# A spectral filter and a ReGLU block on one core: x loaded ahead of the weights, new due times in the head, transform stages in pairs, last columns in three parts

## The chip, the cores and the metric

The kernel runs on one core of a Trainium2 chip. The metric is the device time of one execution in microseconds (us); lower is better. The time before is the median of three runs, 411.16 us (410.84 to 411.76).

## The reference, cut to what matters

```python
def _A_ref(x, w_r, w_i):                      # S = 2048, D = 512
    X = rfft2(x, axes=(-2, -1)) * (w_r + 1j * w_i)
    return irfft2(X, s=(S, D), axes=(-2, -1))

def _B_ref(x, W_gate, W_up, W_down):          # F = 1376
    gate, up = x @ W_gate, x @ W_up
    h = gate * (gate > 0) * up
    return h @ W_down

xn = _layernorm(x)
s = _A_ref(xn, A_w_r, A_w_i)
g = _silu(_B_ref(xn, B_W_gate, B_W_up, B_W_down))
return x + s * g
```

All inputs are float32. Only A_x is used as x. The output is 2048 x 512.

## The kernel before, in words

**Arithmetic.** Every float32 operand of a large product is split into two float16 parts, a high and a low one, and a product is three passes (high by high, high by low, low by high). Weights are first scaled by a power of two that comes from their sum of squares.

**Tiles.** The 2048 rows of x are 16 slices of 128; two slices make a chunk (8 chunks), four make a block (4 blocks). F is cut into 11 tiles of 128 (the last has 96). Gate and up products of one tile of F and one block (`product`) are 12 matmuls of 512 columns into a "gu" PSUM buffer, of which there are two. ScalarE rectifies the gate half (`rectify`), VectorE multiplies it with the up half and splits the result (`hidden`), and the down product (`down`) adds 11 tiles of F for one slice, into a "dn" buffer. `gate` applies the silu on ScalarE.

**Head.** A block's products need its x transposed. For the first two chunks (slices 0 to 3) this is done early: load x (`load_x`), mean and variance on VectorE (`stats`), the reciprocal root (`deviation`: a small VectorE step, a root on ScalarE, a larger VectorE step), normalisation to `xf` (`normalise`), four TensorE transposes of each slice into the PSUM tile `head` (`turn_row`), a copy of the high part to `xT` on ScalarE and of the low part on VectorE. At the same time the weights come in groups (`load_group`, tile `raw`): ScalarE squares them (`squares`), a TensorE matmul with ones sums over partitions (`sum`), VectorE makes the scale `p` (`group_scale`), and the high part is written by ScalarE or VectorE and the low part by VectorE (`group_split`, tile `wgu`). Groups 0, 1 and 2 are one tile of F each. Block 0's first three tiles of F are done for slices 0 and 1 first (12 matmuls of 256 columns for each product), then for slices 2 and 3. Until there is work, TensorE runs dummy matmuls (`keep_busy`, tile `idle`): 60 steps, the first nine of three matmuls, the others of one.

**Transform.** Each chunk is folded (`fold`) and split (`split`), then a first stage of small 64 by 64 matmuls (`first_stage`, tile `s`, 24 matmuls, after which the result goes through DRAM), then eight filter chunks (`fft_chunk`, tiles y, xx, z, v), each with its part on ScalarE, VectorE and GpSimd (tiles `tt`, `po`, `pf`), again through DRAM, then a last stage per chunk (`last_stage`, 24 matmuls into `s`) and the unfolding on GpSimd and VectorE (tiles `ae`, `ye`, `sv`). `finish` multiplies by the silu, adds x and stores. The very last slice is cut by `columns` into two parts of 256 columns, so that the end of the first overlaps the matmuls of the second (tile `dn_3b`).

**What sets the order.** Nothing is issued in the order of the text. Each piece of work is a step of a planner (`Plan`), with an engine, an estimated cost, what it reads and writes, and a due time, its own or derived backwards from its users'. `Plan.run` places steps one by one, on each engine taking of the steps that can begin soonest the one with the earliest due time, with rooms for tiles, one DMA rate of 340 KB/us, 0.095 us for a change of the matmul's shape (`mode`), and a rule that steps marked `port` do not overlap between VectorE and GpSimd. The result is a fixed order for each engine, which the chip keeps. The constants ahead of the functions (T0, FIRST, MID, LAST and their steps, LOADS, LOADX, HIGH_ACT, NORM) are due times and choices of engine. In a trace almost all instructions have the line L64, where the wrapper `InOrder` issues them, so tiles tell them apart.

Of the kernel before, what the change touches and what calls it, by code (L numbers as in the profile page):

```python
# [14 lines left out]
P = 128  # L15
# [3 lines left out]
NCH = 8  # L19
# [51 lines left out]
class Plan:  # L71
# [159 lines left out]
def kernel(ctx: ExitStack, tc: tile.TileContext, x, w_in, wd, wd_tail, wl, ew, sp, c_r, c_d, c_m, c_x, c_s, out):  # L231
# [36 lines left out]
    warm = cpool.tile([P, 1], F32, name="warm")  # L268
    ACT.activation(warm, ones[:, 0:1], AF.Sqrt)
# [21 lines left out]
    def load_x(c):  # L291
        tile_of(f"x{c}", "k4", [P, 2, D], F32)
        for i in range(2) if c == 0 else [None]:
            rows = slice(2 * c, 2 * c + 2) if i is None else slice(i, i + 1)
            to = slice(0, 2) if i is None else slice(i, i + 1)
            step("SP", .6, lambda rows=rows, to=to: SP.dma_start(T[f"x{c}"][:, to], x[:, rows, :]),
                 writes=[(f"x{c}", i)], lead=14 if c else None, kb=512 if i is None else 256, lag=2.2, due=(LOADX[c] + (i or 0) * .01) if c < 2 else None)

    def x_names(c, i):
        return [(f"x{c}", None if c else i)]  # L300

    def stats(c, q, j):
# [7 lines left out]
        for i in range(2):  # L310
            step("DVE", .82, lambda i=i: run(i), reads=x_names(c, i), writes=[(f"st{c}", i), (f"mv{c}", i)])

    def deviation(c):
# [7 lines left out]
        def last():  # L321
# [32 lines left out]
    def normalise(c, q, at, engines=("DVE", "DVE")):  # L354
# [33 lines left out]
    def keep_busy(n):  # L388
# [65 lines left out]
    def first_stage(c, due):  # L454
# [12 lines left out]
        step("PE", SCOST, run, mode=1, reads=["cR", (f"xs16_{c}", 0), (f"xs16_{c}", 1)], writes=[f"s1_{c}"], due=due, margin=MARGIN)  # L467
# [730 lines left out]
```

## Time and profile before

| | before |
|---|---|
| median of 3 runs | 411.16 us (410.84 to 411.76) |
| the profiled execution | 410.83 us, of it 409.1 us span |
| matmuls | 402.5 us busy, 98% of the span |
| VectorE | 306.6 us, 75% |
| ScalarE | 190.0 us, 46% |
| GpSimd | 47.6 us, 12% |
| granted TensorE clock | 0.997 |
| moved by DMA | 51.72 MB |

The span runs from the first to the last instruction of the profiled execution; its device time is 1.7 us longer. PE is TensorE's matmuls, PEld its weight loads, DVE is VectorE, ACT ScalarE, POOL GpSimd, SP the engine that issues most DMAs (SPq its queue of instructions). A row of a timeline gives start, duration, engine, what is written and what is read, and in brackets the idle time before it with what ended it.

### The profile page before, as it was taken

Reading aid. Unit: us, or ns where it says so; the run is one execution under the profiler, and the core shown is the slowest. Engines: PE = TensorE matmul, PEld = TensorE weight load, DVE = VectorE, ACT = ScalarE, POOL = GpSimd, SP = SyncE. Lnnn points to the kernel's source line nnn. Section 1 sums busy time; section 2 is a strip of 40 time slices with the busy share of each in tenths; the row PEclk is TensorE's granted clock in tenths of the full one; section 3 lists DMA queues with packets and bytes.
Section 4 is the critical chain, followed back from the end, with each engine's and each line's share of the span. In section 5 each row is a group of like instructions: output and inputs, shape, how many; then the busy total and the mean of one; then the engine's idle time right before and its main releaser. Section 6 shows DMA issues by size and latency. Waiting matters only on the chain.

```text
span 409.1 us, 7662 instructions
## 1 busy us (share of the span) xinstructions
PE 402.5 (98%) x3023; PEld 213.4 (52%) x3023; DVE 306.6 (75%) x646; ACT 190.0 (46%) x359; POOL 47.6 (12%) x68
## 2 busy tenths in 40 slices
PE   8899999999999999999999999999999999999995
PEld 7784444544444444545465455556455445444554
DVE  3959999999999993515776977878863325999973
ACT  5999655435452549320445434536432327223321
POOL 0000000000000000001230312311311006133320
PEclk9999999999999999999999999999999999999998
DMA  8970210317138269753005144142322089656511
GB/s 285 416 253 6 98 49 3 92 64 154 44 111 145 59 182 355 209 170 116 2 0 168 34 135 125 58 155 57 115 51 53 0 192 221 210 177 211 176 53 52
DMA packets 34948, 51.72 MB, mean 126 GB/s; under 512 B 15392, under 2 KB 17024, under 8 KB 34912
## 3 DMA queue, kind: packets, MB, share of 16 engines
q1 hardware_dynamic: 34624, 50.71, 41.4%
q10 hardware_dynamic: 288, 0.52, 0.5%
q8 instruction: 23, 0.38, 0.4%
q14 instruction: 13, 0.11, 0.1%
HBM read 35.48 MB, written 12.60 MB: 118 GB/s over the span
## 4 chain that ended last, share of the span: by engine, by line
PE 98%; DVE 0%; ACT 0%; issue 0%
PE gu L64 55%; PE dn L64 27%; PE s L64 3%; PE z L64 3%; PE xx L64 3%; PE idle L64 2%; PE y L64 2%; PE v L64 2%; PE dn_3b L64 1%; PE head L64 0%; ACT xT L64 0%; PE sum L64 0%; DVE xT L64 0%; ACT g L64 0%; DVE sv L64 0%
## 5 line engine op out<-in xcount | busy, mean ns | idle before, releaser
L64 PE MATMUL gu<-xT,wgu 128*128 128x512 f16 (+1 forms) x1032 | 214.8, 364 | 1.2 <-ACT xT L64 1.0
L64 PEld LDWEIGHTS <-wgu 128*128 128x128 f16 x1032 | 99.4, 98 | 105.0 <-issue 4.6
L64 PE MATMUL dn<-wds,h 128*128 128x512 f16 (+2 forms) x528 | 115.5, 373 | 0.0
L64 PEld LDWEIGHTS <-h 128*128 128x128 f16 (+1 forms) x561 | 53.7, 98 | 57.7 <-issue 1.8
L64 DVE TENSOR_TENSOR h<-gu,r 128x512 f32<-128x512 f32 (+2 forms) x52 | 33.6, 646 | 26.4 <-PE gu L64 24.5
L64 ACT ACTIVATE h<-h 128x512 f16<-128x512 f32 (+1 forms) x44 | 27.4, 626 | 52.4 <-DVE h L64 50.6
L64 POOL TENSOR_TENSOR po<-tt,tt 128x256 f32<-128x256 f32 x16 | 14.8, 924 | 282.3 <-DVE tt L64 243.2
L64 ACT ACTIVATE r<-gu 128x512 f32<-128x512 f32 (+1 forms) x44 | 26.1, 593 | 30.3 <-PE gu L64 30.0
L64 DVE TENSOR_TENSOR h<-h,h 128x512 f16<-128x512 f32 (+1 forms) x44 | 29.9, 696 | 6.9 <-ACT h L64 6.8
L64 POOL TENSOR_TENSOR ae<-zz 128x128 f32<-128x128 f32 (+1 forms) x32 | 21.3, 698 | 62.5 <-ACT zz L64 43.2
L64 DVE SCALAR_TENSOR_TENSOR tt<-xsp,cw,wt 128x512 f32<-128x512 f32 x32 | 25.6, 863 | 0.0
L64 ACT ACTIVATE g<-dn,cdi 128x512 f32<-128x512 f32 (+1 forms) x16 | 10.3, 673 | 25.9 <-PE dn L64 25.8
L64 DVE TENSOR_TENSOR z<-z,z 128x1024 f16<-128x1024 f32 x8 | 9.8, 1222 | 14.1 <-ACT z L64 14.1
L64 DVE TENSOR_TENSOR sv<-sv,g 128x512 f32<-128x512 f32 (+1 forms) x17 | 11.8, 722 | 7.5 <-ACT g L64 6.9
L64 PE MATMUL gu<-xT,wgt 128*64 128x256 f16 (+1 forms) x144 | 16.9, 309 | 0.0
L64 DVE SCALAR_TENSOR_TENSOR wgu<-raw,p,wgu 128x512 f16<-128x512 f32 x20 | 14.3, 746 | 0.3 <-ACT wgu L64 0.3
L64 ACT ACTIVATE wgu<-raw 128x512 f16<-128x512 f32 x20 | 12.3, 619 | 4.0 <-DMA raw<-in_w 4.0
L64 DVE BATCH_NORM_STATS2 st<-x 128x6 f32<-128x512 f32 x16 | 10.8, 676 | 4.4 <-DMA x<-in_x 4.4
L64 ACT ACTIVATE xs<-xs 128x1024 f16<-128x1024 f32 x8 | 8.4, 1054 | 11.7 <-DVE xs L64 11.7
L64 PEld LDWEIGHTS <-wgt 128*64 128x64 f16 (+1 forms) x144 | 9.6, 106 | 7.4 <-issue 1.7
L64 DVE TENSOR_TENSOR xt<-xt,sv 128x512 f32<-128x512 f32 (+1 forms) x17 | 11.6, 710 | 2.5 <-DMA xt<-in_x 2.3
L64 DVE TENSOR_TENSOR a<-y,a 128x1024 f16<-128x1024 f32 x8 | 9.7, 1217 | 4.9 <-ACT a L64 4.9
(135 smaller groups left out, 431.8 us busy)
## 6 DMA issues: line engine op xcount, KB each, us to landing
A_d<-t SPq DMA_DIRECT2D x16, 256.0 KB, 3.3
rw<-in_wl SPq DMA_DIRECT2D x8, 512.0 KB, 8.7
wt<-in_wl SPq DMA_DIRECT2D x8, 512.0 KB, 4.9
at<-A_d SPq DMA_DIRECT2D x8, 512.0 KB, 5.3
C_d<-t SPq DMA_DIRECT2D x16, 256.0 KB, 3.3
ct<-C_d SPq DMA_DIRECT2D x16, 256.0 KB, 5.9
xt<-in_x SPq DMA_DIRECT2D x16, 256.0 KB, 3.0
out<-xt SPq DMA_DIRECT2D x15, 256.0 KB, 2.1
```

The lines of the kernel that those rows point to most:

```text
L64: return lambda *args, **kw: self.tc.keep_in_program_order(f(*args, **kw))
```

## The change

- **Loads.** The due times put both slices of chunk 0 first, then weight group 0, chunk 1 (now also in two halves), the small constants `cS`, groups 1 and 2. Group 0 is issued by SP instead of ScalarE's queue.
- **Head steps.** A table ORDER gives some 90 steps of the head a due time of their own, in place of the derived one (16 of them below). The normalisation of slice 0 and the high parts of the first halves of tiles 0, 1 and 2 go to GpSimd; slice 3's normalisation goes from VectorE to ScalarE. The root is taken straight from the variance, so the small VectorE step before it and the root no longer follow each other. The low parts of tiles 0 to 2 no longer count as `port`.
- **Pairs.** The first stage of chunks 0 and 1, 2 and 3, 4 and 5, 6 and 7, and the last stage of chunks 0 and 1, 2 and 3, 4 and 5, are planned together: the first of a pair also waits for the second's input. When TensorE is in a special mode, steps of that mode are preferred (STAY).
- **Last columns.** The last slice is cut into 256, 128 and 128 columns.
- **Constants.** All due times of the stages change; the filter chunks are due from 158.38 in steps of 8.85 (before from 179.63 in steps of 14.68), the last stages from 204.61 in steps of 1.35 (before 274.73 and 15.17). Folds no longer wait for their due time less 14.21 (385.05 now). The margin for matmul steps of the transform is 1.2 instead of 1.83.

```diff
-T0, DOWN, FIRST, FIRST_STEP, MID, MID_STEP, LAST, LAST_STEP = 5.52, 50.66, 44.31, 17.14, 179.63, 14.68, 274.73, 15.17
-LOADS, LOADX, LOADU = [8.09, 4.17, 5.72, None, None, None, None], [7.68, 3.63], -2.46
-FOLDS, FOLD_LEAD, MARGIN = [...], 14.21, 1.83
-HIGH_ACT = {(0, 1), (2, 1), (0, 0), (1, 0), (1, 1), (3, 0)}
-NORM, TURN1 = (('ACT', 'ACT'), ('ACT', 'DVE')), 'PE'
-HURRY, SLOW, SLOW_TO = -2.62, 1, 14.66
+T0, DOWN, FIRST, FIRST_STEP, MID, MID_STEP, LAST, LAST_STEP = 10.49, 55.93, 56.31, 14.84, 158.38, 8.85, 204.61, 1.35
+LOADS, LOADX, LOADU = [-28, -24, -22, None, None, None, None], [-30, -26], -25
+FOLDS, FOLD_LEAD, MARGIN = [...], 385.05, 1.2
+HIGH_ACT = {(0, 1), (1, 0), (2, 1), (3, 1), (2, 0), (3, 0)}
+NORM, TURN1 = (('POOL', 'ACT'), ('ACT', 'ACT')), 'PE'
+AHEAD, HIGH_POOL, LOW_POOL, ROWS2, HEAD = 0.87, {(1, 0), (2, 0), (0, 0)}, set(), 2.6, [15.7, 99.0, 9.0, 99.0, 99.0, 99.0, 13.7, 24.4]
+ORDER = {
...
+ "DVE ('mv1', 0)": 23.06, "DVE ('mv1', 1)": 8.01, "DVE ('q0', 2)": -4.94, "POOL ('xf0', 0)": 8.05, "ACT ('xf0', 1)": 12.53,
+ 'PE sum0': 2.84, 'DVE p0': 14.61, "PE ('head0', 0)": 36.32, "PE ('head0', 1)": 27.0,
+ "POOL ('wgu', 0, 0, 0)": 25.53, "DVE ('wgu', 0, 1, 0)": -1.84, "ACT ('wgu', 0, 0, 1)": 16.48, "DVE ('wgu', 0, 1, 1)": 14.54,
+ "PE ('gu0_0_0', 0, 0)": 38.99, "PE ('gu0_0_1', 0, 1)": 7.42, "PE ('gu0_1_1', 0, 1)": 8.43,
...
+HURRY, SLOW, SLOW_TO = -1.89, 1, 30.0
+STAY, PAIR1, PAIR2 = 3., (0, 2, 4, 6), (0, 2, 4)
+BUSY_COST = .46, .115
@@ columns
-    return (slice(0, 256), slice(256, D)) if (c, i) == (NBL - 1, 3) else (slice(0, D),)
+    return (slice(0, 256), slice(256, 384), slice(384, D)) if (c, i) == (NBL - 1, 3) else (slice(0, D),)
@@ Plan.run
+        for s in steps:
+            s.due = ORDER.get(f"{s.engine} {s.names[-1]}", s.due) if s.names else s.due
...
-                    t, s = min((k for k in at if k[0] <= soon), key=lambda k: (k[1].due, k[1].order))
+                    stay = lambda s: STAY if e == "PE" and mode and s.mode == mode else 0.
+                    t, s = min((k for k in at if k[0] <= soon), key=lambda k: (k[1].due - stay(k[1]), k[1].order))
@@ deviation
-        step("ACT", .11, lambda: ACT.activation(T[f"q{c}"][:, 1], T[f"q{c}"][:, 0], AF.Sqrt, scale=-1.0),
-             reads=[f"q{c}"], writes=[(f"q{c}", 1)])
+        step("ACT", .11, lambda: ACT.activation(T[f"q{c}"][:, 1], T[f"mv{c}"][:, :, 1], AF.Sqrt, bias=eps, scale=4.0 / XS ** 2),
+             reads=[(f"mv{c}", 0), (f"mv{c}", 1)], writes=[(f"q{c}", 1)])
@@ normalise
+            if engines[i] == "POOL":
+                POOL.tensor_scalar(to, x, T[f"mv{c}"][:, i, 0:1], at()[:, i:i + 1], op0=ALU.subtract, op1=ALU.mult)
@@ keep_busy
-            at = .43 * min(k, BUSY_COLD) + .11 * max(k - BUSY_COLD, 0)
+            at = BUSY_COST[0] * min(k, BUSY_COLD) + BUSY_COST[1] * max(k - BUSY_COLD, 0)
@@ first_stage
-        step("PE", SCOST, run, mode=1, reads=["cR", (f"xs16_{c}", 0), (f"xs16_{c}", 1)], writes=[f"s1_{c}"], due=due, margin=MARGIN)
+        other = [(f"xs16_{c + 1}", i) for i in range(2)] if c in PAIR1 else []
+        step("PE", SCOST, run, mode=1, reads=["cR", (f"xs16_{c}", 0), (f"xs16_{c}", 1), *other], writes=[f"s1_{c}"], due=due, margin=MARGIN)
@@ load_group
-            e, queue = (("SP", SP), ("ACT", ACT))[g == 0]
-            step(e, .6, lambda i=i, queue=queue: queue.dma_start(...),
-                 writes=[f"raw{g}_{i}"], lead=12 if g else None, kb=2 * w, lag=2.2, due=LOADS[g])
+            step("SP", .6 if g > 2 else .45, lambda i=i: SP.dma_start(...),
+                 writes=[f"raw{g}_{i}"], lead=12 if g else None, kb=2 * w * (AHEAD if g < 3 else 1.), lag=2.2, due=LOADS[g])
@@ group_split
+                if (f, i) in HIGH_POOL:
+                    step("POOL", pool1(512), lambda r=r, high=high, cs=cs, i=i: POOL.tensor_scalar(high, r(i), cs(i), None, op0=ALU.mult), port=True, **names)
@@ last_stage
-        step("PE", SCOST, run, mode=1, reads=[(ctn, 0), (ctn, 1), "cR"], writes=[f"s2_{c}"], due=due, margin=MARGIN)
+        step("PE", SCOST, run, mode=1, reads=[(ctn, 0), (ctn, 1), "cR", *other], writes=[f"s2_{c}"], due=due, margin=MARGIN)
```

`other` in `last_stage` is the input `ct` of chunk c + 1 for c in PAIR2. In `finish`, the reload of x for the last two chunks may be issued up to 20 us ahead of its use instead of 8.

More of the change, by code (lines that the diff above doesn't have):

```diff
@@ L268 @@
     warm = cpool.tile([P, 1], F32, name="warm")
+    eps = cpool.tile([P, 1], F32, name="eps")
+    DVE.memset(eps, 4.0 * EPS / XS ** 2)
     ACT.activation(warm, ones[:, 0:1], AF.Sqrt)
@@ L310, in stats @@
         for i in range(2):
-            step("DVE", .82, lambda i=i: run(i), reads=x_names(c, i), writes=[(f"st{c}", i), (f"mv{c}", i)])
+            step("DVE", .82, lambda i=i: run(i), reads=x_names(c, i), writes=[(f"st{c}", i), (f"mv{c}", i)], due=HEAD[2 * c + 1] + .01 * i if c < 2 else None)
     def deviation(c):
@@ L365, in normalise @@
             e = engines[i]
-            step(e, .62 if e == "ACT" else dve2(512), lambda i=i: run(i), reads=[*x_names(c, i), (f"mv{c}", i), (q, 2)],
-                 writes=[(f"xf{c}", i)], port=e == "DVE")
+            step(e, .62 if e == "ACT" else pool1(512) if e == "POOL" else dve2(512), lambda i=i: run(i), reads=[*x_names(c, i), (f"mv{c}", i), (q, 2)],
+                 writes=[(f"xf{c}", i)], port=e != "ACT", due=HEAD[2 * c] if c < 2 else None)
     def turn(c, lows):
@@ L495, in squares @@
                     junk, T[f"raw{g}_{i}"][:, :, cols], AF.Square, accum_out=T[f"m{g}"][:, 2 * j + i:2 * j + i + 1]),
-                    reads=[f"raw{g}_{i}"], writes=[("wgu", f, 1, i), (f"m{g}", j, i)])
+                    reads=[f"raw{g}_{i}"], writes=[("wgu", f, 1, i), (f"m{g}", j, i)], due=HEAD[4 + g] - .8 if g < 3 else None)
     def group_scale(g):
@@ L503, in group_scale @@
              reads=[(f"m{g}", j, i) for j in range(nf) for i in range(2)], writes=[f"sum{g}"])
-        step("DVE", .52, lambda: scale_of(T[f"sum{g}"][:, :2 * nf], T[f"p{g}"][:, :, :2 * nf], 9), reads=[f"sum{g}"], writes=[f"p{g}"], port=True)
+        step("DVE", .52, lambda: scale_of(T[f"sum{g}"][:, :2 * nf], T[f"p{g}"][:, :, :2 * nf], 9), reads=[f"sum{g}"], writes=[f"p{g}"], port=True,
+             due=HEAD[4 + g] if g < 3 else None)
     def group_split(g):
@@ L705, in product @@
                 cost = pe(12, 256)
-                step("PE", cost, lambda: [part(n) for n in range(3)], reads=[(f"xT{c}", j, h) for j in r for h in range(2)] + weights(f, i), writes=out, due=tick(cost))
+                step("PE", cost, lambda: [part(n) for n in range(3)], reads=[(f"xT{c}", j, h) for j in r for h in range(2)] + weights(f, i), writes=out, due=tick(cost) + (ROWS2 if rows.start else 0.))
             return
@@ L772, in ff_steps @@
         if c == NBL - 1:
-            order = [(f, 2, 0) for f in range(NFT)] + [(f, 3, part) for part in range(2) for f in range(NFT)]
+            order = [(f, 2, 0) for f in range(NFT)] + [(f, 3, part) for part in range(len(columns(c, 3))) for f in range(NFT)]
         else:
@@ L994, in finish @@
         tile_of(n, "k2", [P, D], F32)
-        step("SP", .6, lambda: SP.dma_start(T[n], x[:, 2 * c + i, :]), reads=[(sn, 2)], writes=[(n, "x")], lead=8, kb=256)
+        step("SP", .6, lambda: SP.dma_start(T[n], x[:, 2 * c + i, :]), reads=[(sn, 2)], writes=[(n, "x")], lead=8 if c < 6 else 20, kb=256)
         for part, cols in enumerate(columns(c // 2, j)):
```

57 lines of the change are left out of this document (37 added, 20 removed).

## The prediction, made blind

> **What bounds the kernel now.** I read the page first, for the busy shares.
>
> ```profile
> span 409.1 us, 7662 instructions
> PE 402.5 (98%) x3023; PEld 213.4 (52%) x3023; DVE 306.6 (75%) x646; ACT 190.0 (46%) x359; POOL 47.6 (12%) x68
> ```
>
> TensorE is busy nearly throughout, but part of that may be dummies. So the second view is the list of TensorE's waits, of which the longest behind the first microsecond is this one, and the third is the chain of work that ended last, in order of time (start, duration, what), with one row of the timeline behind it.
>
> ```profile
> PE gu L64 <- ACT xT L64: 1.0, 1, 1.0
> ```
>
> ```profile
> 1.05 6.69 PE idle L64 x46
> 7.74 0.12 PE sum L64 x2
> ...
> 12.21 1.10 ACT xT L64 x2
> ...
> 14.67 2.78 PE gu L64 x24
> ...
> 19.34 0.88 PE head L64 x8
> 20.21 7.86 PE gu L64 x72
> ```
>
> ```profile
> 13.35 1.03 PE L64 MATMUL gu<-xT,wgu 128*128 128x256 f16 x8 [0.96 <-ACT xT L64]
> ```
>
> From 14.67 on the chain is TensorE alone, up to the last matmul just ahead of 404.83 (quoted below). So the span is three terms: a head in which products can't run, a fixed sum of matmul time, and a tail. A faster ScalarE or VectorE in the middle is worth nothing; what counts is when the products begin, how much matmul time isn't arithmetic, and the tail.
>
> How late do products begin, stalls included? One matmul of 256 columns takes 7.86/72 = 0.109 us. Eight were done ahead of 14.67, so without the gap behind them they would have begun at 14.67 - 8 x 0.109 = 13.8. I call this the effective start; the change is measured against 13.8.
>
> **The change part by part: the head.** From the timelines of SP, VectorE and ScalarE I read what the start waits for, and from the DMA issues and one tile's view two durations (KB and us to landing; min, median, max in ns).
>
> ```profile
> 0.73 0.40 SPq L64 DMA_DIRECT2D cS<-in_c_s  x1
> 1.19 0.89 SPq L64 DMA_DIRECT2D x<-in_x  x2
> ```
>
> ```profile
> 6.32 0.69 DVE L64 BATCH_NORM_STATS2 st<-x 128x6 f32<-128x512 f32 x1 [0.41 <-DMA x<-in_x]
> 7.05 0.18 DVE L64 BATCH_NORM_AGGREGATE mv<-st 128x2 f32<-128x6 f32 x1
> ...
> 8.37 0.16 DVE L64 TENSOR_SCALAR q<-mv 128x2 f32<-128x2 f32 x1
> ...
> 9.58 0.16 DVE L64 SCALAR_TENSOR_TENSOR q<-mv,q 128x2 f32<-128x2 f32 x1
> ```
>
> ```profile
> 5.67 0.63 ACT L64 ACTIVATE wgu<-raw 128x512 f16<-128x512 f32 x1 [0.62 <-DMA raw<-in_w]
> 6.21 0.19 ACT L64 ACTIVATION_READ_ACCUMULATOR wgu<-raw 128x1 f32 x1
> ```
>
> ```profile
> xt<-in_x SPq DMA_DIRECT2D x16, 256.0 KB, 3.0
> x<-in_x SPq DMA_DIRECT2D x2, 256.0 KB, 3.8
> ```
>
> ```profile
> L64 ACT ACTIVATE xf<-x,q x3: 800/804/813, 9.9 to 17.6; 128x512 f32<-128x512 f32 x3
> ```
>
> Before, the second half of x lands at 6.32 and the second weight half at 5.67; all share the same DMAs' time. A 256 KB slice takes 3.0 us from issue to landing later in the kernel, 3.8 in this rush. Issued first at 0.73, the first half lands at 3.7 to 4.5, the second at least one issue (0.45, half of 0.89) behind, so 4.2 to 5.2. I take 4.6, nearer the quiet figure since at first nothing runs beside it: 1.7 earlier. Weight group 0, now two issues behind x, I put at 5.9, a little later than its 5.67.
>
> The path of x from there: the statistics end 0.91 after the landing (6.32 to 7.23), at 5.5. From the small step to the last of the reciprocal root it is 8.37 to 9.74, so 1.37; the small step (0.16 and a handover) now runs beside the root, which leaves 1.17, so 6.7. The wait from 7.23 to 8.37, in which VectorE made the scale of the weights, goes too: the scale comes later now. Normalisation: 0.8 on ScalarE for one slice, to 7.5, and for the other GpSimd, which the trace never shows with one input. The nearest rows are in the view of tile `tt`.
>
> ```profile
> L64 DVE SCALAR_TENSOR_TENSOR tt<-xsp,cw,wt x32: 743/746/1223, 191.1 to 305.0; 128x512 f32<-128x512 f32 x32
> L64 POOL TENSOR_TENSOR po<-tt,tt x16: 722/1018/1118, 192.6 to 306.3; 128x256 f32<-128x256 f32 x16
> ```
>
> With two inputs of 256, that is 512 reads, GpSimd takes 0.72 at best and 1.12 at worst; 512 columns could be two of these, 1.44. I take 0.72, since the new step also reads 512; bounds 0.4 (if reads and writes overlap better) and 1.44. So both slices are normalised at 7.5; two transposes of 0.44 (half of 0.88) end at 8.4, the copies to `xT` take 1.10, and x is ready at 9.6 with 0.1 for handovers. Before it was 13.35.
>
> The weights are then as late. Squares of 0.73 (5.67 to 6.40) for the second half end at 6.7, but the sum runs only when the dummies ahead of it are through: 46 of them take 6.69 where the old plan counted 9 x 0.43 + 19 x 0.11 = 5.96, and so the sum sat at 7.74 although its input was there at 6.40. The new costs (0.46, 0.115) give 6.33, still under 6.69, so the sum comes at 7.4 at best. Its scale stands in the table behind chunk 1's statistics (two of 0.87), and ends at 9.0; GpSimd's high part takes 0.72 more, to 9.8 (10.5 with 1.44). With dummies queued ahead, the first product runs at 10.0 to 11.0.
>
> It can't run on freely from there. Between the scale and the last weight of tile 1, VectorE has in a row three low parts of `xT`, the second root's end, a scale, four low parts of weights and a high part.
>
> ```profile
> L64 DVE SCALAR_TENSOR_TENSOR wgu<-raw,p,wgu 128x512 f16<-128x512 f32 x20 | 14.3, 746 | 0.3 <-ACT wgu L64 0.3
> ```
>
> With 0.73 for each of the eight large ones, 0.7 for the root's end (1.37 less the two small steps and the root) and 0.5 for three small scale steps that is 7.0, so the last of tile 1 is there at 16.0 and its product (12 x 0.109 = 1.31) ends at 17.3. By then 48 matmuls (5.23), the transposes of chunk 1 (0.88) and two sums (0.24) are done: an effective start of 17.3 - 6.35 = 10.95. If GpSimd's second high part collides with two low parts (a `tt` takes up to 1.22 instead of 0.75), it is 0.95 more, 11.9. After that TensorE has eight products of 1.31 in hand, over 10 us, while tile 2 and group 3 are made, so I see no further stall. Between the two I take 11.5, a gain of 2.3 us; bounds 0.9 (slow GpSimd and late landing, one after the other) and 3.3.
>
> On that collision the Trainium skill (page "GPSIMD Engine Reference", section "8. Key points") says that GpSimd shares its SBUF interfaces with VectorE, and that the contention is with VectorE instructions in a 2-port mode or with two SBUF inputs. By it the low parts of `xT` (one input in PSUM) go free and only the low parts of the weights pay, which the change no longer marks as `port`; the start would be the 11.9.
>
> **Pairs.** What a visit to the special matmul shape costs is read from the chain around the last stages.
>
> ```profile
> 336.81 0.78 PE s L64 x24
> 337.59 2.70 PE gu L64 x12
> 340.29 1.44 PE s L64 x48
> ...
> 351.79 2.59 PE gu L64 x12
> ```
>
> One stage alone takes 0.78, two in a row 1.44, so the second costs 0.66 and the entry 0.12; the product behind takes 2.70 instead of 2.59, so the exit costs 0.11. One visit fewer is worth 0.23. Before there are 8 visits for the first stages and 7 for the last (one was a pair by chance); after, 4 and at most 5. Six fewer are 1.4 us. A pair waits for its second input, but TensorE is in the middle of hundreds of products there, and they hide it; if the plan ran out of products it would show as a wait of TensorE on `xs` or `ct`. The margin that falls from 1.83 to 1.2 can cost a few tenths where a result comes later than planned; I count 0, bound 0.8.
>
> **Tail.** The end of the timeline, and one VectorE step of 128 columns for comparison.
>
> ```profile
> 404.83 0.47 ACT L64 ACTIVATE g<-dn_3b,cdi 128x256 f32<-128x256 f32 x1 [2.15 <-PE dn_3b L64]
> 405.34 0.43 DVE L64 TENSOR_TENSOR sv<-sv,g 128x256 f32<-128x256 f32 x1 [1.74 <-ACT g L64]
> 405.80 0.42 DVE L64 TENSOR_TENSOR xt<-xt,sv 128x256 f32<-128x256 f32 x1
> ```
>
> ```profile
> L64 DVE TENSOR_TENSOR pf<-po x32: 278/285/821, 197.3 to 309.1; 128x128 f32<-128x128 f32 x32
> ```
>
> With 128 columns each VectorE step falls by 0.14; ScalarE's I take at 0.1: 0.38. Twice 33 matmuls of 128 may cost a little more than 33 of 256; I take 0.1 off for that. Tail: 0.3. The store is half as large; I count nothing for it.
>
> **The sum.** 2.3 + 1.4 + 0.3 = 4.0 us off the profiled execution (409.1 span, 410.83 in all): 406.8. The median of the runs is 0.33 above that execution, so I forecast 407.1 us. All else (the work taken off ScalarE and VectorE, earlier folds, group 0 issued by SP, 0.9 us of issue time before chunk 1) lies beside busy matmuls.
>
> **The rivals.**
>
> *The head gives half or nothing.* Dummies or GpSimd hold the start, or the stall at tile 1 is longer. For it: the sum was held by dummies already, and each engine's order is fixed from estimated times. Against it: x alone has 3.7 us in hand. Head 0.5 to 1: 411.16 - 1.7 - (0.5 to 1) = 408.5 to 409.
>
> *GpSimd starts up slowly.* If its first real step takes L, everything behind the normalisation moves by L - 0.72, less about 1 us of slack. The trace shows no start-up on `po` (1.12 at most over all 16), which speaks against it, but that is another operation. The head's gain is gone at L = 4, all gains at about 6. The Trainium skill (same page, section "2.1 Instruction dispatch") says that the first call of a freshly loaded GpSimd kernel pays about 6 us; by that the result would be about 411.
>
> *The filter chunks crowd VectorE (slower).* They are due 8.85 us apart instead of 14.68.
>
> ```profile
> 54.00:104.00 50.00, 50.00 (x310) 23.34 (x309) 47.49 (x108) 23.82 (x37) 0.00 (x0) 1.00 0.29 74
> 232.00:290.00 58.00, 58.00 (x583) 32.86 (x582) 46.96 (x73) 24.84 (x36) 11.54 (x15) 1.00 0.39 118
> ```
>
> (Stretch, us, then busy time of PE, PEld, DVE, ACT, POOL.) The second stretch holds four chunks by the planned step (58/14.68), and VectorE is busy 46.96, 11.7 us for each chunk and the products beside it. Due every 8.85, it always has work queued, and each `h` multiplication that frees one of the two gu buffers could sit behind a long step (1.22). At 11.7 us for each of eight chunks some 18 tiles of F (5.2 us of products) pass; 0.4 us of wait each is 7 us: 411.16 - 4.0 + 7 = 414. It decides from 0.22 us for each tile. Against it: from 54 to 104 us VectorE is busy 47.49 of 50 and TensorE waits nowhere, so two buffers cover this load when the order is right.
>
> **How the numbers follow.** A measurement of this kernel can tell about 0.2% (0.8 us) from no change. Chances: forecast 0.62 (405.5 to 408.3), half a head 0.22 (408.3 to 410.2), slow GpSimd start 0.06 (same), crowded VectorE 0.10 (slower). Range 405.3 to 410.2: the low end is the head's upper bound (1.0 more) and three or four more chance pairings (0.8); the high end takes in the half head with the margin's 0.8. Faster 0.84, same 0.06, slower 0.10.
>
> **What would show it.** Right: first statistics at about 4, first product at 10 to 11, gaps of under 1.5 us ahead of tile 1's last product, then none; `s` in rows of 48 matmuls of 1.44; VectorE steps of 0.28 at the end. Wrong: a GpSimd step over 1.4 in the head, a wait of TensorE behind 25 us, above all for `h`, or matmul time that isn't some 1.4 us less.

## The result and the profile after

The change makes the kernel slower: a median of 424.61 us (423.55 to 425.48, four runs) against 411.46 us (410.84 to 411.92, four runs) of the kernel before, a ratio of 1.0319 (1.0289 to 1.035). The forecast was 407.1 us. The profiled execution took 423.55 us, of it 421.7 us span. In rows of the changed kernel the line is L69.

The head of the page, and its row of the clock by 40 slices of the span:

```profile
span 421.7 us, 7735 instructions
...
PE 406.9 (96%) x3056; PEld 216.4 (51%) x3056; DVE 304.4 (72%) x647; ACT 188.1 (45%) x358; POOL 58.5 (14%) x72
...
PEclk9999999999999999989999999999999996999999
```

Of the 12.6 us that the span is longer (421.7 less 409.1), TensorE's idle time has 8.2 (421.7 - 406.9 = 14.8, before 6.6) and its busy time 4.4. The clock row is new too: two slices in which TensorE did not get full clock. Before, only the last one falls short:

```profile
PEclk9999999999999999999999999999999999999998
```

The list of TensorE's waits says what the idle time is (us in total, times, longest):

```profile
PE s L69 <- ACT zz L69: 4.0, 1, 4.0
PE y L69 <- DMA at<-A_d: 2.8, 2, 2.5
PE gu L69 <- DVE h L69: 1.5, 1, 1.5
```

Two waits have most of it, and both go back to a load from DRAM. Neither belongs to a part that the prediction costed. Where do they come from? First the one at 183.84, in the timeline of SP's instructions (start, duration; an SP row lasts from when SP takes the instruction to when it can go on):

```profile
168.72 3.02 SPq L69 DMA_DIRECT2D A_d<-t  x4
...
172.44 2.83 SPq L69 DMA_TRANSPOSE xT<-x  x1
...
176.18 3.66 SPq L69 DMA_TRANSPOSE xT<-x  x1
180.02 1.48 SPq L69 DMA_DIRECT2D at<-A_d  x3
```

SP is through with the stores of the first stage (`A_d<-t`) at 171.7. The filter chunk's input `at` is read back from there, and where nothing stands ahead of it, its load goes out 2.95 us behind that row (e1 below: 170.78 to 173.73), so here near 174.7. But two transposing loads stand ahead of it in SP's order and take 2.83 and 3.66 there, and `at` is issued at 180.02; its first part is there at 183.84. The kernel's own plan had `y`, which needs it, at 176.2. TensorE keeps its order and waits 2.55, up to 183.84. Before, no transposing load stood there:

```profile
169.96 1.20 SPq L64 DMA_DIRECT2D A_d<-t  x2
...
175.38 0.91 SPq L64 DMA_DIRECT2D at<-A_d  x2
```

The second, in SP's timeline and in that of all engines:

```profile
325.64 12.45 SPq L69 DMA_DIRECT2D ct<-C_d  x16
338.72 4.32 SPq L69 DMA_DIRECT2D xt<-in_x  x4
```

```profile
348.13 1.33 DVE L69 TENSOR_TENSOR xt<-xt,sv 128x512 f32<-128x512 f32 x2 [3.66 <-DMA xt<-in_x]
...
349.55 1.11 ACT L69 ACTIVATE zz<-s,cwi 128x1024 f32<-128x1024 f32 x1 [5.47 <-DVE xt L69]
...
350.72 1.50 PE L69 MATMUL s<-ct,cR 64*64 64x257 f16 x24 [3.96 <-ACT zz L69]
```

With the last stages due 1.35 us apart, all 16 loads of `ct` (4 MB) go out in one burst. The reload of x for the first chunk, which stands behind them, lands 9.3 us after its issue at 338.72. VectorE's order has the addition of that x next, so VectorE stands for 3.66 until 348.13, ScalarE waits for it, and the next stage `s` waits for the PSUM buffer that ScalarE frees. One late load stops three engines, one after the other.

The clock, from the table by stretches (stretch, us, busy time of PE, PEld, DVE, ACT, POOL, granted clock, DMA share, GB/s):

```profile
183.00:186.00 3.00, 1.89 (x79) 1.69 (x81) 0.20 (x1) 0.75 (x1) 0.00 (x0) 0.87 0.95 318
186.00:189.00 3.00, 3.00 (x42) 1.60 (x37) 2.51 (x4) 1.29 (x2) 0.00 (x0) 0.56 0.99 220
...
348.00:351.00 3.00, 0.28 (x8) 0.28 (x11) 2.77 (x5) 1.45 (x5) 0.00 (x0) 0.68 0.42 152
351.00:354.00 3.00, 3.00 (x29) 1.50 (x22) 2.97 (x7) 2.41 (x7) 1.72 (x3) 0.50 0.65 206
354.00:357.00 3.00, 3.00 (x11) 1.10 (x9) 3.00 (x5) 0.96 (x4) 2.85 (x4) 0.68 0.14 53
```

Behind each wait TensorE works at half clock: 3.4 us behind the first (3 x 0.13 + 3 x 0.44 = 1.7 us lost), 5.2 us behind the second (2.6 lost). That is 4.3 us more. The Trainium skill (page "TensorE: Matmul & The Clock Gate", section "Part 1: The HAM clock gate") says that the array falls to half rate after about one idle window of 3.4 us and returns after a busy one. The trace agrees with half rate and, for the first stretch, with the length; the second lasts 6.8 us, from 349.1, still in the wait, to 355.9. The first wait is shorter than that window, but the clock falls only 1.4 us behind its end (0.13 x 3 / 0.5 = 0.78 ahead of 186), among the small matmuls of `y`, so the runs don't say whether a wait of 2.55 us alone is enough.

The tail did shrink. The last step of ScalarE starts 4.27 us ahead of the end before (404.83 of 409.1); after, 3.62:

```profile
418.08 0.37 ACT L69 ACTIVATE g<-dn_3bb,cdi 128x128 f32<-128x128 f32 x1 [0.64 <-PE dn_3bb L69]
...
418.81 0.29 DVE L69 TENSOR_TENSOR xt<-xt,sv 128x128 f32<-128x128 f32 x1
```

In these two profiles the head gave nothing. To compare heads with different orders I count work: the moment when 48 products' matmuls of 256 columns and all 16 transposes are done. TensorE's timelines, of before and then of after:

```profile
18.74 0.60 PE L64 MATMUL gu<-xT,wgu 128*128 128x256 f16 x4
19.17 1.04 PE L64 MATMUL head<-cS,xf 128*128 128x128 f32 x8
20.05 1.15 PE L64 MATMUL gu<-xT,wgu 128*128 128x256 f16 x9
```

```profile
12.58 0.61 PE L69 MATMUL gu<-xT,wgu 128*128 128x256 f16 x4 [0.22 <-POOL wgu L69]
...
19.18 2.34 PE L69 MATMUL gu<-xT,wgu 128*128 128x256 f16 x20 [0.27 <-DVE xT L69]
```

Before, 48 are done at 20.05. After, 40 are done ahead of 19.18 (4, 12, 4 and 20), so 48 at 19.18 + 8 x 0.109 = 20.05: the same. And GpSimd's four steps in the head:

```profile
8.16 2.08 POOL L69 TENSOR_SCALAR xf<-x,mv,q 128x512 f32<-128x512 f32 x1 [7.73 <-DVE q L69]
10.95 1.57 POOL L69 TENSOR_SCALAR wgu<-raw,p 128x512 f16<-128x512 f32 x1 [0.71 <-DVE p L69]
14.82 2.01 POOL L69 TENSOR_SCALAR wgu<-raw,p 128x512 f16<-128x512 f32 x1 [2.29 <-DVE p L69]
23.30 1.56 POOL L69 TENSOR_SCALAR wgu<-raw,p 128x512 f16<-128x512 f32 x1 [6.48 <-DVE p L69]
```

Last, seven dummies are left over from the head and run between down products, three at 92.35 and four at 93.97, where nothing waits for them (0.77 us, from the differences of starts).

### The profile page after: what moved, and what is told of

Its sections match the earlier page's. It is cut to its first block, busy times and chain, and to the rows that moved or that the text cites. A ratio compares the mean times of both kernels' runs of the same rounds, so it can differ in the third digit from the quotient of the medians.

```text
span 421.7 us, 7735 instructions
## 1 busy us (share of the span) xinstructions
PE 406.9 (96%) x3056; PEld 216.4 (51%) x3056; DVE 304.4 (72%) x647; ACT 188.1 (45%) x358; POOL 58.5 (14%) x72
## 4 chain that ended last, share of the span: by engine, by line
PE 73%; DVE 10%; DMA 8%; ACT 3%; issue 3%; SPq 2%; POOL 0%; DVEq 0%; ACTq 0%; POOLq 0%
PE gu L69 42%; PE dn L69 21%; PE z L69 3%; SPq L69 2%; DMA xt<-in_x 2%; PE xx L69 2%; DVE h L69 2%; DMA ct<-C_d 2%; PE v L69 1%; PE y L69 1%; DVE tt L69 1%; PE s L69 1%; DMA at<-A_d 1%; DVE x L69 1%; ACT t L69 1%
## 5 line engine op out<-in xcount | busy, mean ns | idle before, releaser
L69 PE MATMUL gu<-xT,wgu 128*128 128x512 f16 (+1 forms) x1032 | 216.9, 366 | 2.2 <-DVE h L69 1.5
L69 PEld LDWEIGHTS <-wgu 128*128 128x128 f16 x1032 | 100.1, 99 | 108.4 <-issue 7.9
L69 PE MATMUL dn<-wds,h 128*128 128x512 f16 (+2 forms) x528 | 117.9, 375 | 0.4 <-DVE h L69 0.4
L69 PEld LDWEIGHTS <-h 128*128 128x128 f16 (+1 forms) x594 | 54.2, 98 | 58.2 <-issue 3.6
L69 POOL TENSOR_TENSOR po<-tt,tt 128x256 f32<-128x256 f32 x16 | 15.6, 982 | 247.3 <-ACT xo L69 171.7
L69 ACT ACTIVATE h<-h 128x512 f16<-128x512 f32 (+1 forms) x44 | 27.3, 626 | 49.3 <-DVE h L69 49.3
L69 ACT ACTIVATE r<-gu 128x512 f32<-128x512 f32 (+1 forms) x44 | 26.1, 594 | 50.3 <-PE gu L69 50.2
L69 DVE TENSOR_TENSOR h<-gu,r 128x512 f32<-128x512 f32 (+2 forms) x52 | 33.5, 645 | 19.0 <-PE gu L69 13.7
L69 DVE TENSOR_TENSOR h<-h,h 128x512 f16<-128x512 f32 (+1 forms) x44 | 30.2, 697 | 8.6 <-ACT h L69 8.5
L69 ACT ACTIVATE g<-dn,cdi 128x512 f32<-128x512 f32 (+1 forms) x16 | 10.6, 673 | 41.6 <-PE dn L69 41.6
L69 DVE SCALAR_TENSOR_TENSOR tt<-xsp,cw,wt 128x512 f32<-128x512 f32 x32 | 26.3, 879 | 0.0
L69 POOL TENSOR_TENSOR ae<-zz 128x128 f32<-128x128 f32 (+1 forms) x32 | 20.1, 661 | 37.7 <-ACT zz L69 28.9
L69 DVE TENSOR_TENSOR sv<-sv,g 128x512 f32<-128x512 f32 (+2 forms) x18 | 12.2, 699 | 13.0 <-ACT g L69 12.9
L69 DVE TENSOR_TENSOR a<-y,a 128x1024 f16<-128x1024 f32 x8 | 9.8, 1221 | 13.0 <-ACT a L69 12.8
L69 PE MATMUL gu<-xT,wgt 128*64 128x256 f16 (+1 forms) x144 | 16.9, 309 | 0.0
L69 DVE TENSOR_TENSOR t<-v,t 128x1024 f16<-128x1024 f32 x8 | 9.7, 1222 | 9.9 <-ACT t L69 9.9
L69 POOL TENSOR_TENSOR pf<-tt,tt 128x256 f32<-128x256 f32 x16 | 15.8, 997 | 4.8 <-DVE tt L69 4.2
L69 DVE TENSOR_TENSOR t<-s,t 128x896 f16<-128x896 f32 (+1 forms) x16 | 10.2, 686 | 8.6 <-ACT t L69 8.6
L69 DVE SCALAR_TENSOR_TENSOR wgu<-raw,p,wgu 128x512 f16<-128x512 f32 x20 | 14.7, 768 | 0.3 <-ACT wgu L69 0.2
L69 ACT ACTIVATE a<-y 128x1024 f16<-128x1024 f32 x8 | 8.2, 1023 | 15.0 <-PE y L69 14.3
L69 ACT ACTIVATE xs<-xs 128x1024 f16<-128x1024 f32 x8 | 8.3, 1051 | 14.1 <-DVE xs L69 14.1
L69 PEld LDWEIGHTS <-cR 64*64 64x64 f16 x384 | 10.4, 109 | 7.9 <-issue 7.4
```

Of the source, the lines that this page charges most:

```text
L69: return lambda *args, **kw: self.tc.keep_in_program_order(f(*args, **kw))
```

## The experiments

Two theories. A: the new due times of the stages make an order on SP's queue in which two late loads stop TensorE, and each stop costs clock as well. B: the head, which runs up to 1.3 us late against its plan because of GpSimd, shifts what follows and so makes the waits. Then the parts by themselves. The kernel before took a median of 411.69 beside e1 to e4, 411.54 beside e5 to e8, 411.57 beside e9 to e12 and 411.33 beside e13 and e14; ratios are to it.

**e1_at_first.** After, with two transposing loads behind the loads of `at` in SP's order:

```diff
@@ Plan.run, ahead of the sort of the finished order
+        MOVE = {"('xT2', 3, 1)": 171.1, "('xT3', 1, 1)": 171.2}
+        order = [(MOVE.get(str(s.names[-1]) if s.engine == 'SP' and s.names else None, t), s) for t, s in order]
         order.sort(key=lambda k: k[0])
```

> The changed kernel with one edit: in SP's order two transposing loads of xT (blocks 2 and 3) move behind the three loads of at that they stand ahead of; every other engine keeps its order. Theory A (loads that the new due times put later than the data is wanted): the loads of at go out as soon as A_d is stored, near 175 instead of 180, the wait of TensorE for at (2.55 + 0.26) and the half clock behind it (1.6 lost) go: 424.6 - 4.4 = 420.2, within 1. Theory B (GpSimd's long steps in the head set all later work back by a fixed drift, and the waits follow from that): the wait moves to y or to the next step of the transform, 423.5 to 425.

Measured: 416.13 us, ratio 1.0115 (1.0084 to 1.0146). The wait of `y` is gone and so is the half clock behind it; `at` is issued at 173.73:

```profile
173.73 1.43 SPq L69 DMA_DIRECT2D at<-A_d  x3
175.21 10.29 SPq L69 DMA_TRANSPOSE xT<-x  x2
```

The wait of `s` is still 3.7. By this, the order of two DMAs cost 5.8 us in the profiled executions (421.7 to 415.9) and 8.5 in the median, where theory A had 4.4. The medians differ by more because the clock differs from run to run: after's four runs had a mean clock of 0.987, 0.987, 0.983 and 0.983, and those of e1 took 417.79, 416.59, 415.66 and 415.05 us at 0.991, 0.995, 0.996 and 1.0. These 2.7 us follow the clock; that the three runs without a trace had the same wait is not shown, and the spread of the head (below) is in them too.

**e2_xt_first.** After, with four reloads of x ahead of the burst of `ct`: the same edit with

```diff
+        MOVE = {"('xt0_0', 'x')": 313.91, "('xt0_1', 'x')": 313.92, "('xt1_0', 'x')": 313.93, "('xt1_1', 'x')": 313.94}
```

> The changed kernel with one edit: in SP's order the first four reloads of x (xt of chunks 0 and 1) move ahead of the sixteen loads of ct. Theory A: VectorE's sum for xt no longer waits 3.7 for its load, the copy zz behind it no longer 5.5, TensorE's wait of 3.96 at the last stage and the half clock from 349 to 356 (2.6 lost) go: 424.6 - 6.5 = 418.1, within 1.5. Theory B: the drift stays, TensorE waits elsewhere in the last stage, 422 to 425.

Measured: 418.14 us, ratio 1.0153 (1.0124 to 1.0182), as expected by A. The wait of `s` falls from 4.0 to 0.6 (and another 0.6 for `ct`), and there is no half clock there; the wait of `y` is still 3.3.

**e3_both_no_late_dummies.** Both moves, and no dummies behind 30 us:

```diff
+            if t < 30 or not s.names or s.names[-1] != "idle":
-            s.fn()
+                s.fn()
```

> Both moves together, and the seven dummy matmuls that the plan leaves for 92 to 95 us are not issued (0.77). Theory A: the effects add, 424.6 - 4.4 - 6.5 - 0.8 = 412.9, within 2, and TensorE's waits behind 100 us are under 3 us in all. Theory B: over 418.

Measured: 412.93 us, ratio 1.0037 (1.0015 to 1.006), where theory A said 412.9. The clock is 1.000 over the whole run. What is left of waits behind 25 us, 2.3 in all:

```profile
PE gu L69 <- DVE h L69: 1.1, 1, 1.1
...
PE s L69 <- ACT zz L69: 0.6, 1, 0.6
...
PE dn L69 <- DVE h L69: 0.4, 1, 0.4
...
PE y L69 <- DMA at<-A_d: 0.2, 1, 0.2
```

Six loads moved in SP's order give back 11 of 13 us (424.6 - 0.8 - 412.9), with the head as it was. Theory B falls.

**e4_head_alone.** After with the stage due times, the fold's lead, the margin, the pairs and the columns of before; only the head is new:

```diff
-T0, DOWN, FIRST, FIRST_STEP, MID, MID_STEP, LAST, LAST_STEP = 10.49, 55.93, 56.31, 14.84, 158.38, 8.85, 204.61, 1.35
+T0, DOWN, FIRST, FIRST_STEP, MID, MID_STEP, LAST, LAST_STEP = 10.49, 55.93, 44.31, 17.14, 179.63, 14.68, 274.73, 15.17
-FOLDS, FOLD_LEAD, MARGIN = [...], 385.05, 1.2
+FOLDS, FOLD_LEAD, MARGIN = [...], 14.21, 1.83
-STAY, PAIR1, PAIR2 = 3., (0, 2, 4, 6), (0, 2, 4)
+STAY, PAIR1, PAIR2 = 0., (), ()
-    return (slice(0, 256), slice(256, 384), slice(384, D)) if (c, i) == (NBL - 1, 3) else (slice(0, D),)
+    return (slice(0, 256), slice(256, D)) if (c, i) == (NBL - 1, 3) else (slice(0, D),)
```

> The changed head alone: the changed kernel with the due times of the transform stages, fold lead and margin of before, no pairs, no preference for a special shape, and the last slice in two parts. Theory A: no wait behind 30 us, and as the head gained only 0.1 and the late dummies cost 0.8: 411 to 413, the time of before. Theory B: GpSimd's steps are still there, so the drift is too: over 416.

Measured: 412.88 us, ratio 1.0027 (1.0014 to 1.004), with no wait of TensorE behind 20 us. GpSimd is as late here (a step of 2.08), so that alone makes none of the long waits. The head by itself, with its late dummies, is 0.3% slower than the old one. One comparison with after says what its start depends on. The first squares of ScalarE, which wait for the weights, and the end of the last stall, in e4 and (the first of them) in after:

```profile
6.99 0.63 ACT L69 ACTIVATE wgu<-raw 128x512 f16<-128x512 f32 x1 [4.78 <-DMA raw<-in_w]
...
19.81 2.34 PE L69 MATMUL gu<-xT,wgu 128*128 128x256 f16 x20 [0.28 <-DVE xT L69]
```

```profile
6.36 0.63 ACT L69 ACTIVATE wgu<-raw 128x512 f16<-128x512 f32 x1 [4.14 <-DMA raw<-in_w]
...
6.98 0.28 ACT L69 ACTIVATE q<-mv,eps 128x2 f32<-128x2 f32 x1
```

19.81 - 6.99 and 19.18 - 6.36 are both 12.82, and in e1, e2 and e3 it is 12.82 to 12.90, while the landing moves from 5.62 to 6.99: the whole head hangs on the landing of the weights. The root of chunk 0 (`q<-mv,eps`) stands behind a square in ScalarE's order, though its own input was there at 5.6; that this is the reason is tried in e9.

**e5_last_columns_alone.** Before with the line of `columns` from the change (256, 128, 128) and the loop over its parts.

> The kernel before with the last columns as 256, 128, 128 and nothing else. Theory A: the tail behind the last matmul falls by 0.65 us, as it does in the profile of after (4.25 to 3.6), and twice 33 matmuls of 128 columns cost 33 x (2 x 0.0556 - 0.1092) = 0.07 more: 0.6 us below the kernel before, 410.9 where that takes 411.5, with VectorE steps of 0.29 at the end. Theory B: the time follows the last store's own latency, which the size doesn't change, and the tail only looked shorter: no change.

Measured: 410.85 us, ratio 0.9984 (0.9975 to 0.9993). Theory A: the one part that gains by itself.

**e6_pairs_alone.** Before with STAY, PAIR1, PAIR2 and what they do in `Plan.run`, `first_stage` and `last_stage`.

> The kernel before with the pairs and the 3 us for staying in a shape, its own due times kept. By the plan the stages s fall from 15 visits to 9, and two gaps of TensorE appear, 1.09 at 196 us and 0.65 at 379 us. Theory A, as in my prediction: 0.23 us for each visit, 1.4 off; with the gaps at most 1.7 on: 410.1 to 411.8. Theory B: a visit is worth next to nothing (0.05), since the weight loads beside it take what the entry saves: 411.2 with no gap, up to 413 with both. To be told apart in the trace: time of TensorE from the product ahead of a stage to the product behind it, and the idle time at the two gaps.

Measured: 411.16 us, ratio 0.9994 (0.9985 to 1.0003): no difference that can be told. Visits of `s` fall from 15 to 9 as planned, and a wait comes in their place (the time is where the plan had none; its two gaps did not show):

```profile
PE gu L65 <- DVE h L65: 0.8, 1, 0.8
```

**e7_head_half_gpsimd.** e4 with each GpSimd step cut in two by columns, the second half done by ScalarE:

```diff
-                POOL.tensor_scalar(to, x, T[f"mv{c}"][:, i, 0:1], at()[:, i:i + 1], op0=ALU.subtract, op1=ALU.mult)
+                POOL.tensor_scalar(to[:, 0:256], x[:, 0:256], T[f"mv{c}"][:, i, 0:1], at()[:, i:i + 1], op0=ALU.subtract, op1=ALU.mult)
+                ACT.activation(to[:, 256:D], x[:, 256:D], AF.Identity, bias=T[q][:, 0, i:i + 1], scale=at()[:, i:i + 1])
```

The high parts of the weights are cut in the same way.

> e4_head_alone with one edit: each of GpSimd's four steps in the head does half of its columns, and ScalarE does the other half at the same place of the plan. Theory A: the length of the GpSimd steps (2.08 for xf, 1.57 for the first weight part, against 0.79 planned) eats the head's gain. Then xf and the first weight part take about 1 us or less, the first product starts near 11.5 instead of 12.6, and the time falls by 0.7 to 1.2 us against e4_head_alone: 411.7 to 412.2, ratio about 1.000 to 1.001. Theory B: the dummies and the order of VectorE's steps hold the head: no change from 412.9, ratio 1.003.

Measured: 412.47 us, ratio 1.0022 (1.0013 to 1.003), between the theories and not to be told from e4. The steps did get shorter:

```profile
8.59 1.22 POOL L69 TENSOR_SCALAR xf<-x,mv,q 128x256 f32<-128x256 f32 x1 [8.16 <-DVE q L69]
11.18 0.93 POOL L69 TENSOR_SCALAR wgu<-raw,p 128x256 f16<-128x256 f32 x1 [1.37 <-DVE p L69]
```

but from the weights' landing (6.78) to the end of the last stall (19.21) it still takes 12.43 instead of 12.82. Of 0.9 us that the first step lost, 0.4 arrived.

**e8_columns_and_last_pairs.** Before with the columns of e5 and PAIR2 alone.

> A candidate for the best: the kernel before with the last columns as 256, 128, 128 and pairs among the last stages alone, due times kept. The plan has the same end and one visit of s fewer (15 to 14), no new gap. Theory A: 0.6 for the columns and 0.23 for the visit, 0.8 below the kernel before: 410.7 where that takes 411.5. Theory B, visits are worth next to nothing: 0.6 below, 410.9, the same as e5_last_columns_alone.

Measured: 411.34 us, ratio 0.9993 (0.9984 to 1.0001). No new wait. The interval overlaps that of e5, so the one visit fewer makes no difference that can be told, which speaks for B.

**e9_root_first.** e4 with the root of chunk 0 ahead of both squares, placed like the loads of e1: `"('q0', 1)": 5.0` on ScalarE.

> e4_head_alone with one edit: the root of chunk 0 on ScalarE stands ahead of both squares of weight group 0, where before it stood between them and so waited for the weights' landing (6.99 there, root at 7.62). Theory A: that wait carries the head. The root then ends near 6.0, the reciprocal is done at 6.9 instead of 8.8, GpSimd's step ends near 9 instead of 10.9; the dummies behind the first sum hold the first transposes near 9.6 to 10, so of 1.9 us some 0.5 to 0.7 is left: from the landing of the first weights to the second stall's end 12.2 to 12.3 us instead of 12.82 (19.81 - 6.99), and 412.2 to 412.4, ratio 1.0015. Theory B: the head is bound by ScalarE's own work or the dummies: 12.82 stays, 412.9.

Measured: 412.35 us, ratio 1.0017 (1.0008 to 1.0027). The time is theory A's, though its interval overlaps that of e4, and the way is not. The root runs at 5.59 and GpSimd's step at 6.77 instead of 8.79; yet the last stall ends at 19.63, and the first sum, whose squares were done at 8.14, runs at 9.25: behind 27 dummies.

```profile
5.70 3.71 PE L69 MATMUL idle<-ones 128*128 128x256 f16 x27
9.25 0.28 PE L69 MATMUL sum<-m,ones 128*128 128x2 f32 x2
```

**e10_columns_and_pairs.** Before with the columns of e5 and the pairs of e6.

> Candidate for the best: the kernel before with the two parts of the change that gained by themselves, columns 256, 128, 128 and the pairs with the 3 us for staying; due times and head of before. Theory A, the parts add up: 0.69 and 0.38, 410.5, ratio 0.9975, with a wait for h or the plan's gap of 1.1 us near 196 still in it. Theory B, the gaps that pairing makes eat the rest: 410.9, as e5_last_columns_alone.

Measured: 411.09 us, ratio 0.9987 (0.9976 to 0.9998). Theory B: the pairs add nothing to e5 that can be told; the wait for `h` is 1.3 here.

**e11_head_mended.** e9 with the columns of e5 and without the late dummies.

> e9_root_first with the last columns as 256, 128, 128 and without the seven late dummies. Theory A, three known prices: e9_root_first less 0.77 (dummies at 93 us) less 0.65 (tail): 410.9 if that is 412.3, the same as e5_last_columns_alone, which says that the changed head is by then worth no more than the old one. Theory B: the dummies lay in time that TensorE would have waited anyway: 411.6.

Measured: 411.88 us, ratio 1.001 (0.9999 to 1.0021), nearer to B. Two waits are new in its trace, 0.70 for `h` at 135 us and 0.65 for `at` at 179 us, which is more than the 0.77 that the dummies had taken.

**e12_all_mended.** e3 with the root first as in e9.

> e3_both_no_late_dummies with the root of chunk 0 ahead of the squares: the whole change with all faults mended that the runs found. Theory A: 412.9 less 0.5 from the root, 412.4, still 0.9 above the kernel before, since the new due times leave waits of TensorE behind 25 us (1.1, 0.6, 0.4 and 0.2 there, 2.3 in all). Theory B: with the head in time these waits go too: 410.5 or less.

Measured: 412.09 us, ratio 1.0016 (1.0005 to 1.0027), as A said within 0.3. Its runs lie between 410.24 and 413.17. The profile is of the fastest of them, and shows why beside that of e9. In the table by stretches the number behind PE's busy time is that of matmuls; here the last stretch of e9 with dummies running slowly, and then the one before it of e12:

```profile
6.00:7.00 1.00, 1.00 (x7) 0.72 (x6) 0.75 (x5) 0.72 (x2) 0.23 (x1) 1.00 0.88 248
```

```profile
5.00:6.00 1.00, 1.00 (x12) 0.90 (x10) 0.77 (x4) 0.36 (x2) 0.00 (x0) 1.00 0.97 350
```

The same dummies run at 7 in a microsecond or at 12, and the step comes at 4 us in e12 and at 7 us in e9. With x and the root out of the way, this moment sets when the sum, and all behind it, runs: at 7.71 in e12, at 9.25 in e9.

**e13_fewer_dummies_all** and **e14_fewer_dummies_head.** e12 and e11 without the 11 dummies that the plan puts last ahead of the first sum:

```diff
-            if t < 30 or not s.names or s.names[-1] != "idle":
+            if not s.names or s.names[-1] != "idle" or t < 5.5 or 6.82 < t < 30:
```

> e12_all_mended without the 11 dummies that the plan puts last ahead of the first sum. Theory A: once the root is first, the head waits for the dummies, whose time depends on the moment at which the matmuls of a run become fast (12 in a microsecond instead of 7): from 4 us in e12's profile, where the sum ran at 7.71, and from 6.9 us in e9's, where it ran at 9.25 though its squares were done at 8.14. Without 11 of them the sum runs as soon as its squares are there: 0.25 less in a run like e12's profile, 1.1 less in one like e9's, so 411.3 to 411.7 where e12 took 412.1, with less spread between runs. Theory B: the head is bound by ScalarE and by x, or the clock comes later because TensorE pauses: 412.1 or more.

> The same edit on e11_head_mended (head of the change, last columns, the due times of before). Theory A: 411.0 to 411.5 where e11 took 411.9. Theory B: 411.9 or more. Both stay at or above e5_last_columns_alone (410.9), if the changed head is worth nothing when it is mended.

Measured: 411.58 us, ratio 1.0005 (0.9993 to 1.0018), and 411.25 us, ratio 0.9994 (0.9986 to 1.0003). Both as theory A said (0.5 and 0.6 less than e12 and e11), though differences of that size are near what these runs can tell. The spread of the runs, which was to shrink as well, did in e14 (0.9 us, against 2.3 in e11) and hardly in e13 (2.4, against 2.9 in e12). In e13 the dummies became fast only at about 7 us, as in e9, and still the sum runs at 7.94:

```profile
7.94 0.33 PE L69 MATMUL sum<-m,ones 128*128 128x2 f32 x2
...
18.38 2.35 PE L69 MATMUL gu<-xT,wgu 128*128 128x256 f16 x20 [0.27 <-DVE xT L69]
```

## Why the prediction was wrong, point by point

One ledger for all profiles, each cut into the head (until 48 products' matmuls and 16 transposes are done), the waits of TensorE behind it, late dummies, the tail (from the last ScalarE step's start) and the rest, which is matmul time. For before: 20.05, no waits, no late dummies, 409.1 - 404.83 = 4.27, and 404.83 - 20.05 = 384.78.

| profile | head | waits | late dummies | tail | rest |
|---|---|---|---|---|---|
| before | 20.05 | 0 | 0 | 4.27 | 384.78 |
| e5 columns | 21.32 | 0 | 0 | 3.71 | 384.87 |
| e6 pairs | 20.21 | 0.77 | 0 | 4.16 | 384.26 |
| e8 columns, last pairs | 20.76 | 0 | 0 | 3.69 | 384.85 |
| e10 columns, pairs | 20.05 | 1.26 | 0 | 3.66 | 384.23 |
| after | 20.05 | 8.77 | 0.77 | 3.62 | 388.49 |
| e3 moved loads | 19.90 | 2.29 | 0 | 3.65 | 384.46 |
| e4 head alone | 20.68 | 0 | 0.77 | 4.19 | 385.56 |
| e13 all, fewer dummies | 19.25 | 2.69 | 0 | 3.58 | 384.58 |
| e14 head, fewer dummies | 19.26 | 0.61 | 0 | 3.61 | 385.82 |

- **"All else ... lies beside busy matmuls"**, with the sentence on the pairs that TensorE "is in the middle of hundreds of products there, and they hide it", is the step that failed and cost the sign: 8.8 us of waits and, since after's rest is 4.0 above e3's, some 4 us of clock. The list of what is moved held the new due times of eight stages, and I counted none of their DMAs, neither past which others they go on SP's queue nor that 16 loads become one burst. Shown by e1, e2 and e3.
- **Crowded VectorE** was the rival on the right side, and its price (414) would have been nearer, but it is not what happened: all waits for `h` together are 1.8 us of 8.8 in after, and 1.5 in e3.
- **The head, 2.3 us.** The same kernel's head varies: 20.05 to 21.32 in the five profiles with the old head, mean 20.48, and 19.39 to 20.68 in the five with the head of the change (after, e1 to e4), mean 19.99. The 0.5 between them is no more than the spread of either, so a gain is not shown, and the late dummies cost 0.77. The old head's spread is that of its dummies: in its five profiles the first sum runs between 7.58 and 8.85, and the head ends 12.47 behind it in each. x did land as forecast (second statistics at 4.70, forecast 4.6), but not by the way forecast: it was not issued first. `cS` kept its place, and x went out when it did before (1.19):

```profile
0.72 0.40 SPq L69 DMA_DIRECT2D cS<-in_c_s  x1
1.18 0.88 SPq L69 DMA_DIRECT2D x<-in_x  x2
```

  What is gone is the load of weight group 0 that ScalarE's queue issued at 1.04, ahead of x; that this made the difference was not tried.

  Then three steps of the head failed. (1) GpSimd was taken at 0.72 with 1.44 as the bound; the normalisation takes 2.08, a high part 1.56 alone and 2.01 beside VectorE's low parts. (2) The reciprocal was put at 6.7 because the small step and the root run side by side; I did not look at what stands ahead of the root on ScalarE, and it came at 8.2. (3) The dummies ahead of the sum were put at 7.4 from one profile, where their duration is a matter of the run. No one of them is shown to be the cause alone: e7 mends the first and gains 0.4 us at most, and e9 mends the second, but its profile gains nothing, since the sum ran late. With the root first (e9, e11 to e14) the head ends 11.25 to 11.35 behind the first sum, 1.1 to 1.2 less than the old one, and what is left is when that sum runs: 9.25, 8.60 and 7.71 in e9, e11 and e12, 7.94 and 7.91 in e13 and e14, where 11 dummies fewer stand ahead of it and the head is 1.2 us earlier than the mean of the old. That is the rival "half a head", which I had put at 0.22.
- **Slow start of GpSimd** did not occur: the first step takes 2.08 us, no 6, in each of the ten profiles that have it whole.
- **Contention with VectorE.** The row was a `tt` of 1.22, and the rule that only low parts with two inputs in SBUF pay. Beside GpSimd's step at 14.82 one low part took 0.75, as alone, and the next 1.18, so 0.43 for two where the forecast had 0.95, and GpSimd's own step paid as well (2.01 instead of 1.56). But a later low part of the same form ran wholly beside GpSimd's step at 23.30, and both took what they take alone:

```profile
15.31 1.18 DVE L69 SCALAR_TENSOR_TENSOR wgu<-raw,p,wgu 128x512 f16<-128x512 f32 x1
...
24.05 0.75 DVE L69 SCALAR_TENSOR_TENSOR wgu<-raw,p,wgu 128x512 f16<-128x512 f32 x1
```

  So the rule that the prediction took from the Trainium skill (page "GPSIMD Engine Reference", section "8. Key points") agrees with the first case and not with the second; when such a pair collides stays open. The first step's 2.08 is not contention but its form (two operations, float32 out): in e11 VectorE stood still for 1.36 us of it, between 7.12 and 8.48, and it took the same 2.08 (from 7.03):

```profile
8.48 0.69 DVE L69 BATCH_NORM_STATS2 st<-x 128x6 f32<-128x512 f32 x1 [1.37 <-DMA x<-in_x]
```

- **Pairs, 1.4 us.** The visits fell as forecast, but six visits fewer shorten the rest by 0.5 (e6 against before) or 0.6 (e10 against e5), 0.1 each and not 0.23, and a wait of 0.8 to 1.3 for `h` takes it back. Summed from start to start over e6's trace, `s` itself takes 0.77 us less than before, 0.13 for each visit, as the entry's 0.12 had it. The exit's 0.11, read at one place, is the term that was mis-sized: the long `gu` and `dn` matmuls should have taken 0.66 less and took 0.17 more (0.16 less and 0.33 more). Their order changed too, so this is no price of an exit by itself.
- **Tail, 0.3 us**, was right in kind and too small: 0.55 to 0.65. Half the store was counted at nothing; from the last VectorE step to the end it is 3.30 before (405.80 to 409.1) and 2.89 after, of which VectorE has 0.13.
- **The margin, 0 with a bound of 0.8,** was not tried by itself.

Of the signs of being wrong that the prediction named, all three came: a GpSimd step over 1.4, waits behind 25 us, and matmul time that is 0.3 less and not 1.4 (384.46 in e3).

What stays open: with before's due times the changed head has 0.8 us more matmul time behind it (385.56 in e4, 384.78 before). Summed from start to start, 0.14 of it is one sum that before runs inside its head, and 0.56 lies in the long `gu` and `dn` matmuls, of which 46 instead of 38 stand ahead of a matmul of another tile shape. That fits a price for the change of shape of 0.07 each, but no run tries it. Whether e8 and e10 are really less good than e5 the intervals don't tell.

No combination beats both kernels by more than e5: the kernel before with the last columns as 256, 128 and 128, 0.16% faster (0.07 to 0.25).

## What to carry to other kernels

A due time is an order on every queue that the step uses: before costing new due times at nothing, list each DMA that moves, what it now stands behind on its queue, and which wait of the busiest engine ends with it. Where an engine's order is fixed, one late load stops every engine that has its user next, and a stop of TensorE of 2.5 to 4 us can cost two thirds of that again in clock (4.3 for 6.5 here). Take the price of an operation that no trace shows from above: a GpSimd step with one input was twice the row I chose.

## What the runs showed of the hardware

- GpSimd's TENSOR_SCALAR of 128x512 takes 1.56 us, of 128x256 0.93 (e7), so about 0.3 us and 2.5 ns for each column; VectorE's of the same form takes 0.48 in the same profile:

```profile
20.72 0.48 DVE L69 TENSOR_SCALAR wgu<-raw,p 128x512 f16<-128x512 f32 x1
```

  The Trainium skill (page "GPSIMD Engine Reference", section "4.1 Engine selection") says that with one input GpSimd is roughly at line rate; these rows say a third of VectorE's rate. GpSimd's form with two operations and float32 out (`xf<-x,mv,q`) takes 2.08 us for 512 columns and 1.22 for 256 (e7).
- The moment at which the first matmuls become fast lay between 4 and 7 us (e12, e9) with dummies from 1.05 on, and moved the head of one and the same code by 1.3 us (20.05 in before, 21.32 in e5). The granted clock reads 1.00 in the rows of these stretches; the count of matmuls shows it.
- The clock's fall behind a wait of 3.7 us may not be certain: of e1's four runs one kept 1.0, but only another one was traced, so its wait is not known.
